# Dealing out the output buffers anew: thirteen stores of up to 30 columns in place of seventeen

## The chip, the cores and the metric

The kernel runs on one core of a Trainium2 chip. The metric is the time of one execution on the device in microseconds, as the median of several runs.

## What is computed

For each of four batches, q, k and v are 6400 x 256 in float32. The attention is over channels: a 256 x 256 matrix per batch, from column norms of q and k over all 6400 rows and their product. A small mixture of experts (two of eight, rank 16) is added to the result.

```
qn = q / (norm(q, axis=1) + 1e-6);  kn = k / (norm(k, axis=1) + 1e-6)
a  = softmax(kn.T @ qn / tau)            # 256 x 256 for each batch
x  = v @ a                               # 6400 x 256 for each batch
y  = x + sum over the two best experts e of w_e * (x @ A[e]) @ B[e]
```

## The kernel before, in words

**Columns and tiles.** The 6400 rows of a batch lie over 128 partitions, 50 rows on each, and the code calls these 50 places columns. A column is 256 numbers on 128 partitions. Work on v and on the output goes in tiles of ten columns: tile (b, i) is batch b (0 to 3), piece i (0 to 4), so there are twenty.

**Three stages for each batch.** First q and k are loaded (in two halves of 25 columns, cast to bf16 in the transfer) and PE sums their products into a Gram matrix (`do_G`), while ACT and DVE make the squares for the norms (`do_sq`, `do_add`, `do_red`). Then a short chain makes the matrix a (`do_rsqrt`, `do_exp`, `do_aT`, `do_waA`). Then each tile of v is loaded (also cast), transposed on PE (`do_T`, L976), multiplied for the gate (`do_ZL`, L1000), gated (`m1` to `g2`; `th` is a Tanh on ACT, L1053), and multiplied for the output (`do_Y`, five products of two columns for each tile, L1103 and L1108). `do_Ye` (through `copy`, L956) copies each product from PSUM to the output buffer. PSUM has two banks for the Gram sums and six for all else; a product that waits for its copy holds one of the six.

**Who decides the order.** A planner in Python (`make_plan`, `Plan.run`) lists the steps once; each engine then runs its own in that order and waits on semaphores. A few steps are put elsewhere by hand (`BEHIND`, `TURNS`). The loads are issued by POOL and share queue q0, in their order. The stores are issued by SP (`do_store`, L1119) on queue q1, in their order: SP stands at each until its data is there, and the later stores stand behind it.

**The output buffer.** `Y` has seven slots of ten columns in float32. `at["y", (b, i)]` says which slot a tile gets; the planner deals the slots out, and two tiles that are stored together (`PAIRS`) get neighbours. The first copy of a tile waits until the store that last read its slot has landed. `HOLD` holds a store back until a named load has landed. Slots 0 to 2, 5 and 6 serve other data at the very start.

The stores of before, with the time at which SP issued each and at which it landed (S1 is the first):

| store | tiles | columns | held until | issued | landed |
|---|---|---|---|---|---|
| S1 | (0,4) | 10 | | 116.54 | 129.94 |
| S2 | (0,1) (0,2) | 20 | v(1,3-4) landed | 129.64 | 147.92 |
| S3 | (1,4) | 10 | | 168.00 | 181.74 |
| S4 | (0,3) | 10 | k of batch 3, second half, landed | 180.91 | 193.73 |
| S5 | (1,2) | 10 | the same | 181.29 | 196.64 |
| S6 | (1,0) (1,1) | 20 | v(2,4) landed | 184.64 | 205.70 |
| S7 | (1,3) | 10 | v(3,0-1) landed | 193.61 | 213.03 |
| S8 | (2,2) | 10 | | 205.37 | 218.07 |
| S9 | (0,0) | 10 | v(3,2-3) landed | 210.86 | 221.66 |
| S10 | (2,0) (2,1) | 20 | the same | 211.24 | 227.51 |
| S11 | (2,3) (2,4) | 20 | | 218.44 | 233.55 |
| S12 | (3,0) | 10 | | 224.53 | 236.61 |
| S13 | (3,1) | 10 | | 230.63 | 239.64 |
| S14 | (3,2) | 10 | | 234.45 | 242.67 |
| S15 | (3,3) | 10 | | 239.46 | 245.70 |
| S16 | (3,4), first 6 | 6 | | 242.97 | 247.53 |
| S17 | (3,4), last 4 | 4 | | 244.28 | 248.75 |

Where nothing stands under "held until", or the hold had long ended, the store waited for the last copy of its tiles.

The last loads of before, on POOL:

| load | columns | issued | landed |
|---|---|---|---|
| v(2,0-1) | 20 | 123.19 | 156.90 |
| v(2,2-3) | 20 | 132.39 | 163.31 |
| q of batch 3, second half | 25 | 148.38 | 170.87 |
| k of batch 3, second half | 25 | 148.89 | 180.90 |
| v(2,4) | 10 | 158.85 | 184.63 |
| v(3,0-1) | 20 | 170.26 | 193.55 |
| v(3,2-3) | 20 | 195.94 | 210.84 |
| v(3,4) | 10 | 206.11 | 217.34 |

Of the kernel before, what the change touches and what calls it, by code (L numbers as in the profile page):

```python
# [15 lines left out]
ACT = mybir.ActivationFunctionType  # L16
# [263 lines left out]
def held_by(p, b, i):  # L280

    kind, d, j = HOLD[b, i]
    return [k for k in p.steps if k[:4] == ("load", kind, d, load_of(d, j) if kind == "v" else j)][-1]
# [167 lines left out]
def make_order(words):  # L451

    order = [("qk", 0, i) for i in range(len(QK))]
    for w in words.split():
# [10 lines left out]
HOLD = {(0, 0): ('v', 3, 2), (0, 1): ('v', 1, 4), (0, 2): ('v', 1, 2), (0, 3): ('k', 3, 1), (1, 0): ('v', 2,  # L465
        4), (1, 1): ('k', 3, 2), (1, 2): ('k', 3, 1), (1, 3): ('v', 3, 1), (2, 0): ('v', 3, 3), (2, 1):
        ('k', 2, 0), (2, 2): ('v', 1, 3), (2, 3): ('v', 2, 2), (3, 3): ('v', 2, 2)}
# [7 lines left out]
WHOLE = {(0, 0): 5, (3, 1): 25}  # L475
V_AT = {(3, 0): 0, (3, 1): 1, (3, 2): 2, (3, 3): 3, (3, 4): 0}
BEHIND = {("sq", "q", 1, 3): ("accs", 0, 0), ("red", "k", 3): ("add", "k", 3, 5),
          ("load", "v", 3, 1, 10, 10): ("T", 2, 3, 2)}
TURNS = [[(x, "k", 3, 5), (x, "q", 3, 8), (x, "q", 3, 9)] for x in ("sq", "add")]
SPLIT, SHARES = set(), ()  # L480
OFF = {(0, 0, 'k'), (0, 0, 'q'), (0, 1, 'k'), (0, 2, 'k'), (0, 2, 'q'), (0, 3, 'k'), (0, 4, 'k'), (0, 4,
# [102 lines left out]
def kernel(  # L584
# [11 lines left out]
    nc = tc.nc  # L596
# [3 lines left out]
    CC = C // P  # L600
# [23 lines left out]
    W = {}  # L624
# [3 lines left out]
    def y_slot(n):  # L628
        return Y[:, n * PC:(n + 1) * PC, :]
# [30 lines left out]
    steps = plan.run(HEAD)  # L660
# [5 lines left out]
    for key, other in BEHIND.items():  # L666
        s = next(s for s in steps if s.key == key)
        steps.remove(s)
        steps.insert(next(n for n, x in enumerate(steps) if x.key == other) + 1, s)
    at = {(kind, name): n for s in steps for kind, name, n in s.got}  # L670
    at.update({("v", name): n for name, n in V_AT.items()})
    loaded, waiting = {}, []

    held = {}

    def sb(s, kind, name, shape, dtype, part=""):

        if (kind, name, part) not in held:
            held[kind, name, part] = sbuf.tile(
                shape, dtype, tag=f"{kind}{at[kind, name]}{part}", name=f"{kind}{part}")  # L680
        return held[kind, name, part]
# [5 lines left out]
    st = [dict() for _ in range(B)]  # L687
# [13 lines left out]
    def do_load(s, what, b, i, c, n):  # L701
        if what == "v":
            t, src = VS[:, at["v", (b, c // PC)] * PC:, :], v_v
        elif c + b:
            t = sb(s, "qk", (what, b, i), [P, max(n for _, n in QK), C], BF16)[:, c - QK[i][0]:, :]
            src = {"q": q_v, "k": k_v}[what]
        else:
            sb(s, "qk", (what, b, i), [P, max(n for _, n in QK), C], BF16)
            lo = "qk".index(what) * n
            W[what] = y_slot(0)[:, lo:lo + n, :]  # L710

            early.append((nc.sync if what == "q" else nc.scalar).dma_start(
                W[what], {"q": q_v, "k": k_v}[what][b, :, 0:n, :]))
            return
        r = P
        if what != "v" and (b, i) == REST:
            if c + n == NC:
                t, n, c, r = held["qk", (what, b, i), ""][:, REST_AT - QK[i][0]:, :], NC - REST_AT, REST_AT, FULL
            else:
                n = REST_AT - c  # L720
                for w in "qk" if what == "q" else "":
                    nc.gpsimd.indirect_dma_start(
                        W["side" + w].rearrange("p c d -> p (c d)"), None,
                        {"q": q, "k": k}[w].rearrange("b n d -> (b n d)").rearrange("(m w) -> m w", w=SIDE * C),
                        bass.IndirectOffsetOnAxis(ap=W["slots"], axis=0), bounds_check=B * N // SIDE - 1, oob_is_err=False)
        if what != "v" and (b, i) in WHOLE:
            if c > WHOLE[b, i]:
                loaded[s.key] = loaded[s.key[:4] + PARTS[b, i][-2]]
                return
            n = sum(QK[i]) - c  # L730
        if what == "v" and (b, i) in WITH_NEXT:
            waiting.append((s.key, at["v", (b, c // PC)], c, n))
            return
        keys = [s.key]
        if what == "v" and waiting:
            key, slot, c0, n0 = waiting.pop()
            assert c0 + n0 == c and slot + n0 // PC == at["v", (b, c // PC)]
            t, c, n = VS[:, slot * PC:, :], c0, n0 + n
            keys.append(key)
        name = nc.gpsimd.dma_start(t[0:r, 0:n, :], src[b, 0:r, c:c + n, :]).ins.name  # L740
        for key in keys:
            loaded[key] = name

    def make_side():

# [156 lines left out]

    def do_exp(s, b, ic):

        nc.scalar.activation(st[b]["exp"][:, ic, :].rearrange("i (cc g p) -> i cc g p", cc=CC, g=4),
                             st[b]["accs"][:, ic, :].rearrange("i (p g cc) -> i cc g p", cc=CC, g=4), ACT.Exp,
                             bias=W["neg"][:, 0:1], scale=st[b]["rk"][:, ic:ic + 1],
                             accum_out=st[b]["sum"][:, ic:ic + 1])

    def do_recip(s, b):  # L910
        st[b]["recip"] = bat.tile([P, CC], FP32, name="recip")
# [40 lines left out]
                                    scalar1=st[b]["recip"][:, ic:ic + 1], scalar2=None, op0=OP.mult)  # L952

    def copy(s, out, in_):
        if s.on == "ACT":
            nc.scalar.copy(out, in_)  # L956
        else:
            nc.vector.tensor_copy(out, in_)

    def do_cast(s, what):  # L960
        nc.scalar.copy(held["qk", (what, 0, 0), ""][:, 0:PARTS[0, 0][0][1], :], W[what])
# [26 lines left out]
    def gate_tiles(s, b, i):  # L988
        for part in ("log", "ga", "gb"):
            sb(s, "gate", (b, i), [P, PC, E], FP32, part)  # L990
        for part in ("m1", "m2", "msum"):
            sb(s, "gate", (b, i), [P, PC], FP32, part)
# [30 lines left out]
    def gate_step(name):  # L1023
        def f(s, b, i):
            if (b, i) in MERGED and name == "m1":
                gate_tiles(s, b, i)
            g = {part: held["gate", (b, i), GATE.get(part, part)]
                 for part in ("log", "m1", "eq1", "lm", "m2", "msum", "t", "th", "mask", "g2")}
            if (b, i) in MERGED:
                g["log"] = held["zl", (b, i), ""][:, :, 0:E]  # L1030
            wide = [P, PC, E]
            if name == "m1":
                nc.vector.tensor_reduce(out=g["m1"], in_=g["log"], axis=AX.X, op=OP.max)
            elif name == "eq1":
                nc.vector.tensor_tensor(out=g["eq1"], in0=g["log"], in1=g["m1"].to_broadcast(wide),
                                        op=OP.is_equal)
            elif name == "lm":
                nc.vector.scalar_tensor_tensor(out=g["lm"], in0=g["eq1"], scalar=-1e30, in1=g["log"],
                                               op0=OP.mult, op1=OP.add)
            elif name == "m2":  # L1040
                nc.vector.tensor_reduce(out=g["m2"], in_=g["lm"], axis=AX.X, op=OP.max)
            elif name == "mask":
                nc.vector.tensor_tensor(out=g["mask"], in0=g["log"], in1=g["m2"].to_broadcast(wide),
                                        op=OP.is_ge)
            elif name == "msum":
                nc.vector.tensor_tensor(out=g["msum"], in0=g["m1"], in1=g["m2"], op=OP.add)
            elif name == "t":

                nc.vector.scalar_tensor_tensor(out=g["t"], in0=g["log"], scalar=2.0,
                                               in1=g["msum"].to_broadcast(wide),  # L1050
                                               op0=OP.mult, op1=OP.subtract)
            elif name == "th":
                nc.scalar.activation(g["th"], g["t"], ACT.Tanh, scale=0.5)  # L1053
            else:

                nc.vector.scalar_tensor_tensor(out=g["g2"], in0=g["th"], scalar=1.0, in1=g["mask"],
                                               op0=OP.add, op1=OP.mult)
        return f
# [55 lines left out]
    def do_store(s, b, i, c, n):  # L1114
        lo = i * PC + c
        at_y = at["y", (b, i)] * PC + c
        p = 0
        for rows in SHARES if (b, i) in SPLIT else (P,):
            r = nc.sync.dma_start(out_v[b, p:p + rows, lo:lo + n, :], Y[p:p + rows, at_y:at_y + n, :])  # L1119
            if (b, i) in HOLD and not p:  # L1120
                tc.add_manual_dep(r.ins, loaded[held_by(plan, b, i)],
                                  mybir.DependencyInfo(mybir.DependencyClass.Sync, mybir.DependencyReason.DATA),
                                  reason="held")
            p += rows
# [3 lines left out]
              exp=do_exp, recip=do_recip, aT_ps=do_aT_ps, aT=do_aT, waA_ps=do_waA_ps, waA=do_waA,  # L1128
# [57 lines left out]
```

## Time and profile before

| | us |
|---|---|
| median of 3 runs | 250.2 (250.02 to 250.29) |
| the profiled execution | 250.12 |
| its span on the page (first to last instruction) | 245.8 |
| landing of the last store, from the span's start | 248.75 |

Times in the text are microseconds from the start of the span. The span ends before the last stores land: 248.75 is 2.95 after its end, and 250.12 is 1.37 after that.

| engine | busy us | share of the span |
|---|---|---|
| PE, matmuls | 212.3 | 86% |
| DVE | 185.7 | 76% |
| ACT | 169.2 | 69% |
| POOL | 23.4 | 10% |

The profile cuts the span into 40 slices and gives the busy share of each engine, and of the 16 DMA engines together, in tenths. A DMA packet in it is what one partition's part of a transfer moves; a store or load over 128 partitions has 128 of them, 8 on each DMA engine. For a load the size counted is that of the bf16 written, half of the float32 read. In the timeline a bracket tells how long the engine was idle before the instruction and what released it.

### The profile page before, as it was taken

The numbers are of one execution on the slowest core, as the hardware profiler recorded it, in microseconds if no ns is written. First come the engines' busy times: TensorE is split into PE (matmuls) and PEld (weight loads), VectorE is DVE, ScalarE is ACT, GpSimd is POOL, SyncE is SP. The second block draws the span as 40 slices with busy tenths as digits, with TensorE's granted clock in tenths as the row PEclk, the third lists the DMA queues.
The fourth block names the chain that finished last, engine by engine and source line by source line (L and its number), as shares of the span: only waits on it lengthen the run. The fifth ranks groups of instructions, "written<-read, shape, count | busy, mean of one in ns | idle before, by whom it ended". The sixth has DMA issues, their size and how long they took to land.

```text
span 245.8 us, 5336 instructions
## 1 busy us (share of the span) xinstructions
PE 212.3 (86%) x2203; PEld 177.4 (72%) x2023; DVE 185.7 (76%) x514; ACT 169.2 (69%) x316; POOL 23.4 (10%) x54
## 2 busy tenths in 40 slices
PE   0309797678998999999968999899999999999996
PEld 0207573267777998879858788799775799999985
DVE  1027789447869789999977889998969878788681
ACT  3729341445766769888787668899453599988875
POOL 7700203000030012000100001000000000000000
PEclk9999999569999999999999999999999999999999
DMA  8999999999999999999999999999999999999999
GB/s 280 218 210 218 215 222 219 209 219 223 206 218 217 221 204 221 223 210 210 257 292 240 337 280 210 218 216 223 277 248 290 401 373 282 313 421 435 406 425 424
DMA packets 7872, 65.93 MB, mean 268 GB/s; under 512 B 1088, under 2 KB 1472, under 8 KB 3368
## 3 DMA queue, kind: packets, MB, share of 16 engines
q0 software_dynamic: 4864, 38.67, 75.0%
q1 hardware_dynamic: 2648, 26.13, 25.6%
q10 hardware_dynamic: 336, 0.79, 0.8%
q8 instruction: 16, 0.26, 0.4%
q14 instruction: 8, 0.07, 0.1%
HBM read 79.90 MB, written 26.21 MB: 432 GB/s over the span
## 4 chain that ended last, share of the span: by engine, by line
DMA 47%; PE 33%; issue 9%; POOL 4%; DVE 4%; ACT 2%; POOLq 0%
DMA v<-in_v_dram 37%; DMA qk<-in_k_dram 10%; PE Y_ps L1103 9%; PE T_ps L976 5%; PE ZL_ps L1000 5%; PE Y_ps L1108 4%; PE acc L785 4%; PE gzT_ps L1090 3%; POOL qk L740 2%; DVE ssq L819 2%; DVE gz L1078 1%; PE acc L789 1%; PE acc L793 1%; ACT y L956 1%; ACT sq L812 1%
## 5 line engine op out<-in xcount | busy, mean ns | idle before, releaser
L785 PE MATMUL acc<-qk 128*128 128x256 bf16 (+1 forms) x400 | 75.4, 284 | 19.8 <-DMA qk<-in_k_dram 11.6
L785 PEld LDWEIGHTS <-qk 128*128 128x128 bf16 (+1 forms) x400 | 38.9, 103 | 32.1 <-DMA qk<-in_k_dram 12.7
L956 ACT COPY y<-Y_ps 128x512 f32<-128x512 f32 x87 | 50.7, 594 | 15.2 <-PE Y_ps L1108 12.8
L1103 PE MATMUL Y_ps<-a_bf,vT 128*128 128x256 bf16 x400 | 60.0, 272 | 0.0
L1103 PEld LDWEIGHTS <-vT 128*128 128x128 bf16 x400 | 38.3, 98 | 4.8 <-issue 0.2
L819 DVE TENSOR_TENSOR ssq<-ssq,sq 128x1280 f32<-128x1280 f32 x25 | 37.2, 1487 | 3.8 <-ACT sq L812 3.7
L1108 PE MATMUL Y_ps<-ball,gzT 128*128 128x256 bf16 x200 | 38.2, 273 | 0.0
L812 ACT ACTIVATE sq<-qk 128x1280 f32<-128x1280 bf16 x25 | 32.1, 1285 | 8.0 <-DVE ssq L819 7.6
L1078 DVE TENSOR_TENSOR gz<-zl,gatega 128x256 bf16<-128x256 f32 x95 | 35.4, 445 | 0.5
L789 PE MATMUL acc<-qk 128*128 128x128 bf16 (+1 forms) x170 | 31.2, 220 | 0.0
L976 PE MATMUL T_ps<-ident,v 128*128 128x128 f32 x200 | 25.8, 275 | 5.8 <-DMA v<-in_v_dram 5.6
L793 PE MATMUL acc<-qk 128*128 128x128 bf16 (+1 forms) x200 | 28.6, 226 | 0.0
L976 PEld LDWEIGHTS T_ps<-ident,v 128*128 128x128 f32 x200 | 21.7, 141 | 7.3 <-issue 4.6
L819 DVE TENSOR_TENSOR ssq<-ssq,y 128x1280 f32<-128x1280 f32 (+1 forms) x10 | 14.8, 1491 | 16.0 <-ACT y L812 15.6
L956 ACT COPY vT<-T_ps 128x512 f32<-128x512 f32 (+1 forms) x47 | 22.7, 547 | 5.9 <-PE T_ps L976 5.6
L1000 PE MATMUL ZL_ps<-waA_sb,vT 128*128 128x136 bf16 x380 | 26.3, 223 | 0.5 <-ACT y L956 0.3
L1000 PEld LDWEIGHTS <-vT 128*128 128x128 bf16 x380 | 23.8, 98 | 1.5 <-DVE gz L1078 0.5
L793 PEld LDWEIGHTS <-qk 128*128 128x128 bf16 (+1 forms) x200 | 19.0, 102 | 4.8
L956 ACT COPY zl<-ZL_ps 128x408 f32<-128x408 f32 (+1 forms) x50 | 19.9, 457 | 3.4 <-PE ZL_ps L1000 3.4
L1090 PE MATMUL gzT_ps<-ident,gz 128*128 128x128 f32 x100 | 19.6, 280 | 2.0 <-DVE gz L1078 1.7
L1108 PEld LDWEIGHTS <-gzT 128*128 128x128 bf16 x200 | 19.5, 98 | 2.3
L812 ACT ACTIVATE y<-qk 128x1280 f32<-128x1280 bf16 (+1 forms) x10 | 12.2, 1263 | 11.4 <-DMA qk<-in_k_dram 8.1
(93 smaller groups left out, 234.9 us busy)
## 6 DMA issues: line engine op xcount, KB each, us to landing
out_dram<-y SPq DMA_DIRECT2D x11, 1280.0 KB, 12.7
out_dram<-y SPq DMA_DIRECT2D x4, 2560.0 KB, 17.3
qk<-in_q_dram POOLq DMA_DIRECT2D x6, 1600.0 KB, 18.1
qk<-in_k_dram POOLq DMA_DIRECT2D x6, 1600.0 KB, 25.4
v<-in_v_dram POOLq DMA_DIRECT2D x6, 1280.0 KB, 29.7
v<-in_v_dram POOLq DMA_DIRECT2D x8, 640.0 KB, 25.6
qk<-in_q_dram POOLq DMA_DIRECT2D x1, 1280.0 KB, 10.9
qk<-in_k_dram POOLq DMA_DIRECT2D x1, 1280.0 KB, 16.4
```

The source lines that it names most:

```text
L785: nc.tensor.matmul(acc[ic][:, 0:256], kt[0:r, j, ic::CC], qt[0:r, j, :], start=c == 0, stop=False, skip_group_check=True)
L789: nc.tensor.matmul(acc[ic][:, 256:384], kt[0:r, j, ic::CC], kt[0:r, j, ic::CC], start=False, stop=False, skip_group_check=True)
L793: nc.tensor.matmul(acc[ic][:, 384:512], qt[0:r, j, ic * P:(ic + 1) * P], qt[0:r, j, ic * P:(ic + 1) * P], start=False, stop=c == NC - 1, s ...
L812: nc.scalar.activation(out[0:r, 0:n, :], t[0:r, j:j + n, :], ACT.Square)
L819: nc.vector.tensor_tensor(out=t, in0=t, in1=held["sq", (w, b, g), ""][0:r, 0:n, :], op=OP.add)
L956: nc.scalar.copy(out, in_)
L976: nc.tensor.matmul(ps[:, j, :], vt[:, c + j, :].bitcast(FP32), W["ident32"], is_transpose=True, start=(j == 0), stop=(j == n - 1))
L1000: nc.tensor.matmul(ps[:, j, :], vT_of(b, i, c + j)[:, :, ic], st[b]["waA"][:, ic, :], start=(j == 0 and ic == 0), stop=(j == n - 1 and ic ...
L1078: nc.vector.tensor_tensor(out=pairs[:, h].rearrange("p c (e r) -> p c e r", e=E), in0=z[:, 2 * h:2 * h + 2, :].rearrange("p c (e r) -> p c ...
L1090: nc.tensor.matmul(ps[:, j, :], pairs[:, j * P:(j + 1) * P], W["ident32"], is_transpose=True, start=(j == 0), stop=(j == n // 2 - 1))
L1103: nc.tensor.matmul(ps[:, j, :], vT_of(b, i, c + j)[:, :, ic], st[b]["a"][:, ic, :], start=(j == 0 and ic == 0), stop=False, skip_group_che ...
L1108: nc.tensor.matmul(ps[:, j, :], pair[:, :, j], W["B"], start=False, stop=(j == 1), skip_group_check=True)
```

## The change

Slots, sizes and holds of the stores are set by hand, on top of the planner's order. `Y_AT` gives each tile a slot. `GOES` renames a store step of the planner (its place in the order stays) or drops it. `AFTER` makes a store, or one load, wait for the end of a named load or of a named ACT instruction; `made` remembers those instructions. The orders of the instructions on PE, DVE and ACT, and those of the loads on POOL, stay as they were; what differs there is which semaphores some copies wait for.

| store | tiles | columns | slots | held until |
|---|---|---|---|---|
| A1 | (0,0) | 10 | 2 | v(1,1) landed |
| A2 | (0,1) (0,2) | 20 | 3, 4 | v(1,3-4) landed |
| A3 | (0,3) (0,4) | 20 | 5, 6 | `th` of tile (2,2) done |
| A4 | (1,0) (1,1) | 20 | 0, 1 | the same |
| A5 | (1,2) (1,3) | 20 | 2, 3 | `exp` of batch 3, first half, done |
| A6 | (1,4) | 10 | 4 | v(3,2-3) landed |
| A7 | (2,0) (2,1) | 20 | 5, 6 | the same |
| A8 | (2,2) (2,3) (2,4) | 30 | 0, 1, 2 | its data |
| A9 | (3,0) (3,1) | 20 | 3, 4 | its data |
| A10 | (3,2) | 10 | 5 | its data |
| A11 | (3,3) | 10 | 6 | its data |
| A12, A13 | (3,4) | 6, 4 | 0 | its data |

One load is held too: v(3,0-1), which waited for the last transpose out of its slots before, now waits for `th` of tile (2,3) as well.

```diff
 BEHIND = {("sq", "q", 1, 3): ("accs", 0, 0), ("red", "k", 3): ("add", "k", 3, 5),
-          ("load", "v", 3, 1, 10, 10): ("T", 2, 3, 2)}
+          ("load", "v", 3, 1, 10, 10): ("th", 2, 3), ("store", 1, 3, 0, 10): ("exp", 3, 0)}
+Y_AT = {(0, 0): 2, (0, 1): 3, (0, 2): 4, (0, 3): 5, (0, 4): 6, (1, 0): 0, (1, 1): 1, (1, 2): 2, (1, 3): 3, (1, 4): 4,
+        (2, 0): 5, (2, 1): 6, (2, 2): 0, (2, 3): 1, (2, 4): 2, (3, 0): 3, (3, 1): 4, (3, 2): 5, (3, 3): 6, (3, 4): 0}
+GOES = {(0, 4): (0, 0, 0, 10), (1, 4): None, (0, 3): (0, 3, 0, 20), (1, 2): None, (1, 3): (1, 2, 0, 20),
+        (2, 2): (1, 4, 0, 10), (0, 0): None, (2, 3): (2, 2, 0, 30), (3, 0): None, (3, 1): (3, 0, 0, 20)}
+AFTER = {("store", 0, 0): ("load", "v", 1, 1, 10, 10), ("store", 0, 3): ("th", 2, 2), ("store", 1, 2): ("exp", 3, 0), ("store", 1, 0): ("th", 2, 2),
+         ("store", 1, 4): ("load", "v", 3, 2, 20, 20), ("load", "v", 3, 1): ("th", 2, 3)}
...
+    for s in list(steps):
+        if s.key[0] == "store" and s.key[1:3] in GOES:
+            if GOES[s.key[1:3]]:
+                s.key = ("store",) + GOES[s.key[1:3]]
+            else:
+                steps.remove(s)
     at = {(kind, name): n for s in steps for kind, name, n in s.got}
     at.update({("v", name): n for name, n in V_AT.items()})
-    loaded, waiting = {}, []
+    at.update({("y", name): n for name, n in Y_AT.items()})
+    loaded, waiting, made = {}, [], {}
+
+    def behind(ins, key):
+        if key in AFTER:
+            other = AFTER[key]
+            tc.add_manual_dep(ins, loaded[other] if other[0] == "load" else made[other],
+                              mybir.DependencyInfo(mybir.DependencyClass.Sync, mybir.DependencyReason.DATA), reason="held")
+        return key in AFTER
...
-        name = nc.gpsimd.dma_start(t[0:r, 0:n, :], src[b, 0:r, c:c + n, :]).ins.name
+        ins = nc.gpsimd.dma_start(t[0:r, 0:n, :], src[b, 0:r, c:c + n, :]).ins
+        behind(ins, s.key[:4])
         for key in keys:
-            loaded[key] = name
+            loaded[key] = ins.name
...
             r = nc.sync.dma_start(out_v[b, p:p + rows, lo:lo + n, :], Y[p:p + rows, at_y:at_y + n, :])
-            if (b, i) in HOLD and not p:
+            if not behind(r.ins, s.key[:3]) and (b, i) in HOLD:
                 tc.add_manual_dep(r.ins, loaded[held_by(plan, b, i)],
```

`do_exp`, `copy` and the `th` branch of `gate_step` change only in that they note the name of their instruction in `made`.

More of the change, by code (lines that the diff above doesn't have):

```diff
@@ L903, in do_exp @@
     def do_exp(s, b, ic):
[L905 to L908, printed above, removed]
+        made[s.key] = nc.scalar.activation(
+            st[b]["exp"][:, ic, :].rearrange("i (cc g p) -> i cc g p", cc=CC, g=4),
+            st[b]["accs"][:, ic, :].rearrange("i (p g cc) -> i cc g p", cc=CC, g=4), ACT.Exp, bias=W["neg"][:, 0:1],
+            scale=st[b]["rk"][:, ic:ic + 1], accum_out=st[b]["sum"][:, ic:ic + 1]).ins.name
     def do_recip(s, b):
@@ L954, in copy @@
     def copy(s, out, in_):
[L955 to L958, printed above, removed]
+        r = nc.scalar.copy(out, in_) if s.on == "ACT" else nc.vector.tensor_copy(out, in_)
+        made[s.key] = r.ins.name
     def do_cast(s, what):
@@ L1052, in f @@
             elif name == "th":
-                nc.scalar.activation(g["th"], g["t"], ACT.Tanh, scale=0.5)
+                made[s.key] = nc.scalar.activation(g["th"], g["t"], ACT.Tanh, scale=0.5).ins.name
             else:
```

## The prediction

> **What bounds the kernel now.** I read first the page's DMA lines, then PE's waits from 157.5 on, then the stores one by one.
>
> ```profile
> DMA  8999999999999999999999999999999999999999
> GB/s 280 218 210 218 215 222 219 209 219 223 206 218 217 221 204 221 223 210 210 257 292 240 337 280 210 218 216 223 277 248 290 401 373 282 313 421 435 406 425 424
> ...
> q0 software_dynamic: 4864, 38.67, 75.0%
> q1 hardware_dynamic: 2648, 26.13, 25.6%
> ...
> DMA 47%; PE 33%; issue 9%; POOL 4%; DVE 4%; ACT 2%; POOLq 0%
> ```
>
> The 16 DMA engines are full in every slice but the first. q0 (loads, counted at half their float32 bytes) and q1 (stores) take 75.0% and 25.6%, together the whole span. So the last landing, 248.75, is the sum of all transfers: a store moved elsewhere moves others, and the end stays unless bytes pass faster or the engines run dry.
>
> PE is the second bound. Its last wait for data in the timeline, and all its waits from 157.5 to 244:
>
> ```profile
> 157.03 1.06 PE L976 MATMUL T_ps<-ident,v 128*128 128x128 f32 x8 [1.00 <-DMA v<-in_v_dram]
> ```
> ```profile
> PE gzT_ps L1090 <- DVE gz L1078: 0.6, 2, 0.4
> PE ZL_ps L1000 <- DVE gz L1078: 0.2, 1, 0.2
> ```
>
> After v(2,0-1) lands PE waits 0.8 us in 87 us, and not for a load. What comes late to PE there moves its end, but the stores lag PE: S15 is issued at 239.46, when S13 (239.64) and S14 (242.67) have not landed. I estimate that PE may come 1 us later (0 to 1.2) before the end moves: S17 lands 4.47 after its issue and 1.22 after S16, so 0 to 3 us of the 4.47 are queueing.
>
> **Fewer, larger stores.** Four stores go. The price of a merge comes from landings one behind the other when no load runs: S12 to S15, ten columns each, land 3.03 apart (236.61, 239.64, 242.67, 245.70); S11, twenty columns, lands 6.04 after S10. Two small ones cost 6.06, one large one 6.04: 0.02 saved, for four merges 0.1. The other end: S12 took 3.06, and S10 landed 5.85 after S9, so 0.27 a merge, 1.1 for four. These rows exclude a loss for twenty columns. Thirty no row shows; three tens are 9.09, one and a half twenties 9.06, so it is taken as free. I take 0.1: S10 to S11 is clean of loads, while S9 and S10 were queued when the last load had just ended. SP's issues (0.33 each) lie beside full DMA engines and cost nothing either way.
>
> **Loads and stores at once.** By the DMA view, 40 to 110 (loads only) moved 15.08 MB counted, 30.2 of float32, in 70 us: 431 GB/s. 218 to 233 (stores only, mostly of twenty columns) moved 6.39 MB: 426. 170 to 218, mixed and mostly ten-column stores: 5.34 doubled and 9.60 MB in 48 us, 422. 133 to 146, a twenty-column store against 25-column loads:
>
> ```profile
> q0 software_dynamic: 127, 1.42, 51.4%
> q1 hardware_dynamic: 128, 2.62, 47.7%
> ```
>
> That is 5.46 MB in 13 us, 420. At 431 the stretch 170 to 218 would be 1.0 us shorter, at 420 it would be 0.2 longer. The changed kernel mixes as long but with larger packets; I take -0.1 and keep +0.2 and -1.0.
>
> The same two lines show 127 load packets against 128 store packets: the queues take turns packet by packet, so a twenty-column packet against the same load packet takes a larger share than a ten-column one, and loads beside it are slower. The Trainium skill ("DMA: Bandwidth & Descriptors", Queues, rings and completion order) says that each engine goes round its queues and empties a whole packet of some 9 to 17 descriptors before it switches. With the eight rows that a store has on an engine, a store would go in one turn by that; the trace, at 127 to 128 over 13 us, shows turns of one row.
>
> **Stores and loads that move.** A1 leaves after v(1,1) lands at 117.21 instead of 116.54, A2 at v(1,3-4) as before: the same 30 columns precede v(2,0-1), so 156.90 stands. S3 (168.00) is gone; A3 and A4 start when `th` of (2,2) ends (172.13 + 0.25). A step of each transfer alone: 25 columns 7.55 (163.31 to 170.87), twenty loaded 6.1 (71.65 to 77.78), ten loaded 3.07 (68.58 to 71.65), twenty stored 6.04. k's second half follows q's (170.87): alone it would land at 178.4. A3's first packets come some 3.5 later than its issue (the prefetched loads are ahead, an estimate: at 133, 3.4 after S2's issue, both queues flow), at 176; the last 2.4 us of k at half share take 4.6, so it lands near 180.6 (180.90 before). v(2,4) then alternates with A3: 188 to 190 instead of 184.63, but PE transposes it only at 194.00. v(3,0-1) is issued at `th` of (2,3), 185.91 + 0.25, instead of 170.26. The sum 170.87 + 7.55 + 6.04 + 3.07 + 6.04 + 6.1 puts its landing at 199.7 instead of 193.55; PE wants it at 204.6. On POOL v(3,2-3) stands behind it and goes when its slots are free, as before:
>
> ```profile
> 195.94 0.53 POOL L740 DMA_DIRECT2D v<-in_v_dram  x1 [25.15 <-PE T_ps L976]
> ```
>
> It lands at 207 to 210 (210.84 before), v(3,4) near 217.5 as before. No load reaches PE late.
>
> **New waits of copies.** The first copy of (2,0) now waits for A3, issued 172.4; sharing as above, it lands near 187.5. The first copy is at 186.63 on ACT:
>
> ```profile
> 186.63 0.59 ACT L956 COPY y<-Y_ps 128x512 f32<-128x512 f32 x1
> 193.08 0.37 ACT L841 COPY acc_sb<-acc 128x256 f32<-128x256 f32 x1 [5.86 <-PE acc L789]
> ```
>
> Behind it ACT idles 5.86 anyway, and its PSUM bank is next taken at 192.89 (L834): about 1 us of waiting is hidden; the cover ends near 192. (2,2) waits for A4 (195 to 198.5), its copy is at 199.94. (2,4) waits for A5, issued at 199.5 when `exp` ends: 3.5 to start, 6.04 of its own, 2 to 4 of loads in between, 0.7 to land: 212.2 to 214.3. Its first copy is the one at 214.02:
>
> ```profile
> 214.02 1.24 ACT L956 COPY y<-Y_ps 128x512 f32<-128x512 f32 x2
> 215.43 0.81 ACT L956 COPY zl<-ZL_ps 128x408 f32<-128x408 f32 x2 [0.17 <-PE ZL_ps L1000]
> ```
>
> The bank is taken again by the third product of the tile, at 215.7, so a landing until 215.0 costs PE nothing. The others have 5 us and more. A9 waits for both its tiles, until 230.63, where S12 went at 224.53. 50 columns stand from it to the end, as from S12; all before S12 landed at 233.55, and its data was through some 0.6 earlier. With 1.5 from issue to flow A9 is there at 232.1, 0.8 early.
>
> **Sum.** Merges -0.1, mixture -0.1, waits and dry queues 0: 250.12 - 0.2 = 249.9 (248.0 with both gains at their ends, 250.2 with neither). The profiled execution lies 0.08 below the median 250.2. What can be told from no change is about 0.2%, 0.5 us; so: no change.
>
> **Rivals.**
> *The transfers pass faster.* Merges at 0.13 (midway) save 0.5, and half the gain of an unmixed stretch another 0.5: 249.1. For it: 422 GB/s against 431. Against: the landings 3.03 and 6.04, and that A3 to A7 still run against loads. That it goes beyond 249.1 I give 0.08 of its chance. 0.25.
> *Tile (2,4) waits for A5* (slower). One store of twenty columns lands 15.1 to 21.1 after its issue before (S11, S6), if queued behind others; at 18.3 (S2, alone in q1 against loads) A5 would land at 217.8, ACT would stand 3.8 at the copy with the zl copies, the gate and the other y copies behind it, PE would lose 2.8 and, less 1 of spare, the end 1.8: 251.9. At 217 it is 251.1. It decides from 215.0, the end moves from 216. Against: less load work beside A5 than beside S2. 0.15.
> *The queues run dry* (slower). v(3,0-1) is through near 199.1 and v(3,2-3), issued 195.94, must flow by then; A9 must by 232.9. Each has about 0.8 of spare; if PE or the loads are off by 1.8 at one, the DMA engines stand for 1 us that nothing gives back: 250.9. 0.12.
> *A whole store in one turn.* A3 and A4, 12.1 together, would pass ahead of k: 178.4 + 12.1 = 190.5, while PE starts on it near 183.5 (25 columns of 0.33 before 193.05, and 1.2 of other work): 7 less 1 of spare, 255.9. The page's rule above would do that; the packet counts speak against it. 0.01.
>
> **How the numbers follow.** The forecast has 0.47. Faster by over 0.5 us: 0.25. Slower by over 0.5: 0.15 + 0.12 + 0.01 = 0.28. The range goes from 249.1, the faster rival, to 251.1, the tile wait at 217 and the dry queue; below lie 0.08 and above about 0.1. The forecast's own range is 249.7 to 250.4.
>
> **What would show it right or wrong.** Right: thirteen stores, DMA at 9 in every slice, PE's waits after 157.5 near 1 us, k's second half at 180 to 181, A5 landed before 215, the first copy of (2,0) waiting under 2 us. Wrong: a gap on PE after 214 ended by an ACT copy (the tile wait), DMA slices under 9 near 199 or 232 (dry), or landings of the pure stores less than 3.0 per ten columns (faster).

## The result, and the profile after

The changed kernel takes 251.97 us (median of 6 runs, 251.62 to 252.52), the kernel before 250.12 (6 runs, 250.02 to 250.29): a ratio of 1.0075, 95% interval 1.0062 to 1.0088. It is 1.9 us slower, beyond the range of the prediction (249.1 to 251.1). The profiled execution took 251.81; its span is 246.0, and its last store lands at 250.46, 1.71 later than before.

First the page of the changed kernel, the lines that answer to those shown of before: the busy share of the DMA engines and the rate in 40 slices of 6.15 us, the two queues, the chain.

```profile
DMA  8999999999999999999999999999999999999999
GB/s 280 217 211 216 211 226 221 206 221 219 210 221 216 217 206 223 217 218 206 243 289 276 325 271 215 216 218 219 256 357 398 267 197 322 338 407 438 422 411 424
...
q0 software_dynamic: 4864, 38.67, 75.4%
q1 hardware_dynamic: 2023, 25.83, 25.1%
...
PE 42%; DMA 36%; issue 9%; DVE 6%; POOL 4%; ACT 3%; POOLq 0%
```

The DMA engines are at 9 in every slice but the first, as before, and the packets of both queues again take the whole span (75.4 and 25.1%). By this line nothing is lost, and yet the last store lands later. One slice of the rate stands out: the 33rd, 196.8 to 202.9, with 197 GB/s. In slices 2 to 19, before the first store, the rate of loads alone is 206 to 226.

Next the waits of PE from 157.5 to 250, and two stretches of ACT in the timeline, around the first copies of (2,0) and of (2,4):

```profile
PE gzT_ps L1109 <- DVE gz L1097: 0.6, 2, 0.4
PE Y_ps L1122 <- DVE zl L976: 0.2, 1, 0.2
```
```profile
187.00 0.59 ACT L976 COPY y<-Y_ps 128x512 f32<-128x512 f32 x1
193.40 0.37 ACT L862 COPY acc_sb<-acc 128x256 f32<-128x256 f32 x1 [5.82 <-PE acc L810]
...
214.34 1.24 ACT L976 COPY y<-Y_ps 128x512 f32<-128x512 f32 x2
215.75 0.81 ACT L976 COPY zl<-ZL_ps 128x408 f32<-128x408 f32 x2 [0.17 <-PE ZL_ps L1019]
```

PE waits 0.8 us, as before. The copy of (2,0) is at 187.00 (186.63 before) and that of (2,4) at 214.34 (214.02), neither with an idle time in front of it. The computation is where it was, some 0.3 later; what is late is the stores. A13 is issued at 244.60 and lands at 250.46, 5.86 later, where S17 took 4.47.

Now the stretch of the low slice, in the view by windows: the last two columns are the mean busy share of the DMA engines and the GB/s. First before, then after.

```profile
196.00:200.00 4.00, 4.00 (x39) 3.61 (x38) 2.53 (x10) 3.83 (x9) 0.46 (x1) 1.00 1.01 427
200.00:204.00 4.00, 4.00 (x52) 3.75 (x50) 3.80 (x12) 3.63 (x10) 0.00 (x0) 1.00 1.01 294
```
```profile
196.00:200.00 4.00, 4.00 (x39) 3.62 (x38) 2.46 (x11) 3.82 (x10) 0.53 (x1) 1.00 1.01 204
200.00:204.00 4.00, 4.00 (x52) 3.75 (x50) 4.00 (x12) 3.67 (x10) 0.00 (x0) 1.00 1.03 174
```

The rates can't be compared across these rows as they stand, since a load counts half of its float32 bytes. The DMA view of 196 to 204 splits them by queue (packets, MB, share of the 16 engines), before and after:

```profile
q1 hardware_dynamic: 128, 2.32, 68.5%
q0 software_dynamic: 53, 0.54, 32.0%
```
```profile
q0 software_dynamic: 162, 1.50, 101.5%
q1 hardware_dynamic: 1, 0.00, 0.0%
```

In float32 that is 2.32 + 2 x 0.54 = 3.40 MB in 8 us before, 425 GB/s, and 3.00 MB after, 375. The 0.40 MB that are missing cost 0.94 us at 425. In the changed kernel no store flows here: the data of A4 is through at 195.5, and A5, issued at 199.85, moves its first packet at 204.05. What flows is the end of v(3,0-1), which lands at 199.57, and v(3,2-3), issued at 196.25:

```profile
196.25 0.53 POOL L760 DMA_DIRECT2D v<-in_v_dram  x1 [8.95 <-PE T_ps L995]
```

The trace's packets show two things. First, some engines stand for a moment. With 16 engines, fewer than 16 packets in flight means that at least one has none; in the kernel before that does not happen from 190 to 244, and in the changed kernel 15 and at the lowest 14 are in flight at times between 197.0 and 203.3. What is missing adds up to 1.3 us of one engine, less than 0.1 us of all sixteen, too little to show in the slices. Second, and this is most of it, the packets take longer. One partition's row of a twenty-column load takes 0.78 us in the mean in the kernel before (190 to 211). In the changed kernel the 147 rows that start between 196 and 204.6 take 0.89, and the 38 of them from 201.5 on 1.10, up to 1.41.

The other part of the 1.71 us is at the end. The packets of a store are spread over 16 engines, and it lands when the slowest is done. By the completions of the last store in the trace, the mean engine was done at 249.20, against 248.32 before: 0.88 later, near the 0.94 above. It was done 1.26 before the slowest, against 0.43 before: 0.83 more, which makes up the 1.71. Where this uneven end comes from is open. Slow packets are not needed for it: E1 and E10 below move 428 and 429 GB/s over 196 to 208, and still their mean engine ends 0.75 and 1.40 before the slowest. In E10 the engines had even been level at 220, where the completions of A6 lie within 0.19.

### The profile page after: what moved, and what is told of

It is laid out like the page before. It is cut to its first block, busy times and chain, and to the rows that moved or that the text cites. A ratio compares the mean times of both kernels' runs of the same rounds, so it can differ in the third digit from the quotient of the medians.

```text
span 246.0 us, 5327 instructions
## 1 busy us (share of the span) xinstructions
PE 214.8 (87%) x2203; PEld 179.5 (73%) x2023; DVE 184.9 (75%) x514; ACT 169.0 (69%) x316; POOL 23.7 (10%) x54
## 3 DMA queue, kind: packets, MB, share of 16 engines
q0 software_dynamic: 4864, 38.67, 75.4%
q1 hardware_dynamic: 2023, 25.83, 25.1%
## 4 chain that ended last, share of the span: by engine, by line
PE 42%; DMA 36%; issue 9%; DVE 6%; POOL 4%; ACT 3%; POOLq 0%
DMA v<-in_v_dram 28%; PE Y_ps L1122 11%; DMA qk<-in_k_dram 8%; PE acc L806 6%; PE T_ps L995 6%; PE Y_ps L1127 5%; PE ZL_ps L1019 5%; PE gzT_ps L1109 3%; PE acc L810 2%; DVE gz L1097 2%; DVE ssq L840 2%; POOL qk L760 1%; PE acc L814 1%; ACT y L976 1%; ACT zl L976 0%
## 5 line engine op out<-in xcount | busy, mean ns | idle before, releaser
L806 PE MATMUL acc<-qk 128*128 128x256 bf16 (+1 forms) x400 | 76.3, 287 | 19.3 <-DMA qk<-in_k_dram 11.2
L806 PEld LDWEIGHTS <-qk 128*128 128x128 bf16 (+1 forms) x400 | 39.4, 104 | 31.8 <-DMA qk<-in_k_dram 12.1
L995 PE MATMUL T_ps<-ident,v 128*128 128x128 f32 x200 | 27.4, 286 | 3.7 <-DMA v<-in_v_dram 3.3
L995 PEld LDWEIGHTS T_ps<-ident,v 128*128 128x128 f32 x200 | 23.2, 147 | 5.0 <-issue 4.1
L814 PEld LDWEIGHTS <-qk 128*128 128x128 bf16 (+1 forms) x200 | 19.2, 103 | 4.9
## 6 DMA issues: line engine op xcount, KB each, us to landing
qk<-in_k_dram POOLq DMA_DIRECT2D x6, 1600.0 KB, 25.1
```

Source lines behind the costliest of these rows:

```text
L806: nc.tensor.matmul(acc[ic][:, 0:256], kt[0:r, j, ic::CC], qt[0:r, j, :], start=c == 0, stop=False, skip_group_check=True)
L814: nc.tensor.matmul(acc[ic][:, 384:512], qt[0:r, j, ic * P:(ic + 1) * P], qt[0:r, j, ic * P:(ic + 1) * P], start=False, stop=c == NC - 1, s ...
L995: nc.tensor.matmul(ps[:, j, :], vt[:, c + j, :].bitcast(FP32), W["ident32"], is_transpose=True, start=(j == 0), stop=(j == n - 1))
```

## Experiments

Each kernel was timed beside the kernel before, whose median there was 250.41 for E1 to E7 and 250.52 for E8 to E10; ratios are to that. The views are of one execution of each. Theories named in the expectations: **L**, any load without a store beside it is slow; **S**, the large stores are dear in themselves; **W**, waits of the computation set the time. Later **T** and **D** came in place of L: T, the tail of a load with nothing behind it and nothing beside it is slow; D, a load that starts on engines which have nearly run dry, with no store beside it, is slow.

**E1: A5 issued earlier.** One hold is changed; A5 goes at 186.36 instead of 199.85.

```diff
-("store", 1, 2): ("exp", 3, 0)
+("store", 1, 2): ("th", 2, 3)
```

> The changed kernel, but A5 waits for th of tile (2,3) (near 187) instead of exp of batch 3 (near 200); it is then queued behind A4. Theory L (the load v(3,2-3) crosses with no store beside it, its packets are slow, and the DMA engines lose about 1.0 us between 196 and 204): that stretch moves near 427 GB/s of float32 again instead of 380, and the time falls by 1.0 to 1.7, to 250.3 to 251.0; some may come back at v(3,4), which then crosses with little beside it. Theory S (stores of 20 and 30 columns are dear in themselves, one DMA engine falling behind on them): no change, 251.9. Theory W (waits on the compute engines): no change, 251.9.

Measured: 250.32 (250.09 to 250.74), ratio 1.0000, interval 0.9991 to 1.0010. The whole loss is gone, with the same thirteen stores, so S and W, which both said 251.9, fall, and what the loss needs is the place of A5 in time. The DMA view of E1 over 196 to 204:

```profile
q1 hardware_dynamic: 93, 1.80, 53.1%
q0 software_dynamic: 96, 0.82, 48.7%
```

3.44 MB in 8 us, 430 GB/s. But L has a first crack here. Once the data of A5 is through (207.8), E1's loads run alone too, and the row of the windows shows them at 209 GB/s, 418 in float32, where the changed kernel had 174:

```profile
208.00:212.00 4.00, 4.00 (x48) 3.75 (x46) 2.71 (x9) 3.27 (x7) 0.00 (x0) 1.00 1.01 209
```

**E2: A5 and A6 both earlier.** A6, too, no longer waits for v(3,2-3); it goes when `exp` ends.

```diff
-("store", 1, 2): ("exp", 3, 0), ("store", 1, 4): ("load", "v", 3, 2, 20, 20)
+("store", 1, 2): ("th", 2, 3), ("store", 1, 4): ("exp", 3, 0)
```

> As the run before, and A6 waits for exp of batch 3 instead of the landing of v(3,2-3), so that a store stands in the queue beside every load to the end. Theory L: 250.0 to 250.4, as the kernel before the change. Theory S or W: 251.9.

Measured: 251.40 (251.27 to 252.04), 1.0045 (1.0028 to 1.0061). The slow stretch is gone, but the time is not back, and no theory had forecast it. Stores now take a share from the loads as long as they last; v(3,2-3) lands at 214.07 instead of 208.86, and PE waits for it:

```profile
PE T_ps L995 <- DMA v<-in_v_dram: 2.4, 2, 1.6
```

The last store is issued at 246.44, 1.84 later. So the cure has a limit on the other side: too many stores beside the loads make PE the late one.

**E3: the stores from A3 on in pieces of ten columns**, one behind the other at the same holds; the pieces of A8 and A9 go as their tiles are ready, so the first of A8 leaves before its last tile is there.

```diff
-r = nc.sync.dma_start(out_v[b, p:p + rows, lo:lo + n, :], Y[p:p + rows, at_y:at_y + n, :])
+step = n if (b, i) == (0, 1) else PC
+for x in range(0, n, step):
+    m = min(step, n - x)
+    r = nc.sync.dma_start(out_v[b, p:p + rows, lo + x:lo + x + m, :], Y[p:p + rows, at_y + x:at_y + x + m, :])
```

> The changed kernel with its slots and holds, but every store from A3 on goes out in pieces of ten columns, one behind the other at the same releases (A8 and A9 in pieces as their tiles are ready). Theory S: back to 250.1 to 250.6. Theory L: the lone crossing of v(3,2-3) stays, 251.7 to 252.2, with 196 to 204 near 380 GB/s.

Measured: 252.18 (251.98 to 252.33), 1.0072 (1.0056 to 1.0089). Small stores lose as much as large ones: S is refuted again.

**E4: v(3,2-3) as two loads of ten columns**, issued one behind the other.

```diff
-ins = nc.gpsimd.dma_start(t[0:r, 0:n, :], src[b, 0:r, c:c + n, :]).ins
+if s.key[:4] == ("load", "v", 3, 2):
+    nc.gpsimd.dma_start(t[0:r, 0:PC, :], src[b, 0:r, c:c + PC, :])
+    ins = nc.gpsimd.dma_start(t[0:r, PC:n, :], src[b, 0:r, c + PC:c + n, :]).ins
```

> The changed kernel, but v(3,2-3) goes as two loads of ten columns issued one behind the other. If the slow packets come from there being one single transfer on the queue (nothing to fetch ahead), a second load behind it should help and the time falls by 0.5 or more, to 251.4 or less; if they come from loads alone after the engines ran dry, whatever their number, it stays at 251.7 to 252.2.

Measured: 252.06 (251.82 to 252.74), 1.0076 (1.0056 to 1.0097). Nothing is won by two loads: it is no matter of how a single large transfer is cut.

**E5: ten columns from A5 into A4.** Still thirteen stores and the same moments of issue; A4 has thirty columns and A5 ten.

```diff
-(1, 3): (1, 2, 0, 20)
+(1, 3): (1, 3, 0, 10), (1, 0): (1, 0, 0, 30)
-("store", 1, 2): ("exp", 3, 0)
+("store", 1, 3): ("exp", 3, 0)
```

> The ten columns of tile (1,2) move from A5 into A4, so A4 is thirty columns, issued at 173.25, and A5 ten, issued at 199.85 as before this edit. The same bytes go out; 3 us more of stores flow ahead of 199, so v(3,0-1) should land near 202.5 instead of 199.57, with v(3,2-3) (issued 196.25) already queued behind it, and A5 should begin near 203.5 to 204. So loads still run alone for some 3 us, near 200.5 to 204, but the tail of the one has the next behind it. Theory T (a load loses speed only in its last 3 us, where nothing is queued behind it and no store runs beside it): 250.1 to 250.7, with 425 to 430 GB/s in 196 to 204. Theory L (any load without a store beside it is slow): 251.3 to 252.0, with 380 to 400 GB/s where the loads are alone.

Measured: 250.53 (250.33 to 251.46), 1.0006 (0.9996 to 1.0016). The loss is gone from the median, although A5 goes no earlier (199.85). The profiled execution is the slowest of the ten (251.46): PE waited 1.0 there for a copy on DVE, and the last store was issued at 245.76, 1.16 later than in the changed kernel. Its load stretch shows no slow packets all the same. There v(3,0-1) lands at 203.17, so v(3,2-3), issued at 196.25, finds the queue full. Between 200 and 203 the loads run alone, at 2 x 0.65 MB in 3 us, 433 GB/s:

```profile
q0 software_dynamic: 79, 0.65, 102.4%
q1 hardware_dynamic: 5, 0.00, 0.2%
```

L is refuted: being alone does not make a load slow. (The loads alone over 40 to 110 before, at 431, had said so already.) But most of these rows are of v(3,0-1), issued at 186.78, whose mean engine is done at 202.2; v(3,2-3) is alone for a short time only, since A5 flows from 203.2.

**E6: the hold of v(3,0-1) undone**; that load is issued at 170.34 again.

```diff
-("load", "v", 3, 1, 10, 10): ("th", 2, 3)
+("load", "v", 3, 1, 10, 10): ("T", 2, 3, 2)
-("load", "v", 3, 1): ("th", 2, 3)
```

> The changed kernel with only the hold of v(3,0-1) undone: it waits again for the last transpose out of its slots, and is issued near 170. Theory H (the hold of the load makes the loss): 250.0 to 250.5. Theories T and L: what is issued by 196 is the same sum and is moved by about 199.5 in either order; v(3,2-3), issued near 196, begins near 200 and has no store beside it until A5 begins near 203.5. Under L 251.5 to 252.0 (3.5 us at about 380 GB/s lose 0.4, engines with nothing to move near 199.5 as much again). Under T its tail lies beside A5, and the loss is less: 250.7 to 251.4.

Measured: 251.70 (251.45 to 252.25), 1.0061 (1.0044 to 1.0078). Most of the loss stays, so the hold of the load is not its cause. Only the order of the same work changed: v(3,0-1) landed at 199.88, v(3,2-3) was issued at 195.98, and no store flowed until 203.0. T had expected 250.7 to 251.4 and missed.

**E7: A5 issued some 4 us earlier**, at 195.61, held by a copy of the transposes of tile (2,4), which ends near that time.

```diff
-("store", 1, 2): ("exp", 3, 0)
+("store", 1, 2): ("Te", 2, 4, 0)
```

> The changed kernel with A5 held by the copy of tile (2,4) on ACT that ends near 195.7 instead of by the exp that ends near 199.8: A5 is issued near 196, 3.9 earlier, and begins near 199.5, together with v(3,2-3). The tail of v(3,0-1), 197 to 199.5, is still alone; the tail of v(3,2-3) has A5 beside it. T and L: most of the loss returns, 250.1 to 250.8, with 400 to 425 GB/s in 196 to 204. Theory W (the time is set by waits on PE and the copies, not by the transfers): unchanged, 251.8 to 252.2.

Measured: 251.13 (250.46 to 251.59), 1.0035 (1.0023 to 1.0048). About half of the loss is won back, less than expected. The profiled run is the fastest of the six (250.46) and shows no slow packets, with A5 flowing from 197.2. It can't say what the slower runs lost. That stays open.

**E8 and E9: one more load behind v(3,2-3).** Ten columns of v are read again, into a buffer of k that nobody reads any more. E8 is the changed kernel with that load, E9 is E1 with it.

```diff
+if s.key[:3] == ("load", "v", 3) and c == 20:
+    nc.gpsimd.dma_start(held["qk", ("k", 3, 1), ""][:, 0:10, :], v_v[3, :, 40:50, :])
```

> The changed kernel with one more load of ten columns issued right behind v(3,2-3); it reads rows of v again into a buffer of k that nobody reads any more. The output stays the same; the bytes cost 3.0 us (ten columns). v(3,2-3) still starts on an empty queue with no store beside it, but its tail now has a load behind it. Theory T (the tail of a load with nothing behind it and nothing beside it is slow): 425 to 430 GB/s in 200 to 204, and the loss of the change goes: 253.0 to 253.8, that is 250.1 plus 3.0 and a few tenths. Theory D (a load that starts on engines that have run dry, with no store beside it, is slow): 360 to 400 GB/s in 200 to 204, 254.4 to 255.0.

> The control for the run before: the kernel whose A5 is held by th of tile (2,3), with the same redundant load behind v(3,2-3). T and D: it had no loss, so only the bytes count: 250.3 plus 3.0, 253.1 to 253.6. If the redundant load costs more than its bytes (v(3,4) comes 3 us later to PE), it shows here, and the run before is read against this one.

Measured: E8 254.80 (254.04 to 256.06), 1.0163 (1.0146 to 1.0181); E9 253.13 (253.04 to 253.37), 1.0109 (1.0092 to 1.0126). The control pays for its bytes (2.8 more than E1). E8 is 1.67 above it; the changed kernel, from another session, is 1.65 above E1. The loss has not moved, though the tail of v(3,2-3) now has a load behind it. T is refuted; D had expected 254.4 to 255.0. The row of E8 by windows:

```profile
200.00:204.00 4.00, 4.00 (x49) 3.72 (x47) 4.00 (x12) 3.66 (x10) 0.00 (x0) 1.00 1.04 177
```

A full share and 177 GB/s again; from 198 to 200 up to four of the engines stand. The 131 twenty-column rows that start from 197.5 to 206 take 0.97 us in the mean, up to 1.8; from 206 on, A5 having flowed since 205.0, they take 0.78 again. The additional load comes later: its rows start at 208.2 and take the usual 0.40 of ten columns. This profile is of the slowest of the four executions (256.06, in which PE waited 1.8 for a load), so its numbers are the far end of E8.

**E10: a lone tail in another place.** E1, with A6 waiting for v(3,4), the last load, so that nothing runs beside that load's end.

```diff
-("store", 1, 4): ("load", "v", 3, 2, 20, 20)
+("store", 1, 4): ("load", "v", 3, 3, 40, 10)
+BEHIND: ("store", 2, 2, 0, 10): ("load", "v", 3, 3, 40, 10)
```

> The kernel whose A5 is held by th of tile (2,3) has no loss. Here its A6 (and with it A7, behind it on SP) waits for v(3,4), the last load, in place of v(3,2-3): A6 is issued near 215 in place of 211.9, so that the last 3 us of v(3,4), 212 to 215, have nothing behind them and no store beside them. T: the slow tail comes back at this place, 330 to 400 GB/s in 212 to 215 where 425 was, and v(3,4) lands near 215.5. Theory P (the slowness belongs to v(3,2-3) or to 196 to 204, not to a lone tail): 425 there, v(3,4) lands at 214.7 to 215.0. In both, the engines then stand for some 3.4 us until A6 begins, and all later stores come that much later: 253.5 to 254.0 under P, 254.0 to 255.0 under T.

Measured: 253.46 (253.29 to 253.71), 1.0118 (1.0101 to 1.0135), and v(3,4) lands at 215.51. By its time this is P, by the landing T. Over 212 to 215 the queue moved 0.43 MB, 287 GB/s in float32, even less than T expected. The rows by windows say of what kind that is:

```profile
208.00:212.00 4.00, 4.00 (x48) 3.71 (x47) 2.75 (x9) 3.31 (x8) 0.00 (x0) 1.00 0.98 205
212.00:216.00 4.00, 4.00 (x45) 3.69 (x43) 3.52 (x13) 3.71 (x10) 0.00 (x0) 1.00 0.52 106
```

The rate falls here with the busy share (0.98 to 0.52): the engines finish at different times and then stand, and every row of v(3,4) takes the usual 0.40 us of ten columns. That is how a queue that runs dry looks. In the changed kernel the share stayed at 1.03 while the rate was 174.

**All runs by one measure.** "Lead" is the time from the issue of v(3,2-3) to the landing of the load ahead of it. The rate is in float32 over 196 to 208, from the trace's packets, each one's bytes spread evenly over its duration (the DMA view counts a packet where it starts, which shifts a stretch by up to 0.3 MB at an edge).

| kernel | lead, us | store beside it in 200 to 203 | GB/s | time |
|---|---|---|---|---|
| before | -2.4 | yes | 428 | 250.1 to 250.5 |
| after | 3.3 | no | 389 | 251.97 |
| E3 | 3.6 | no | 397 | 252.18 |
| E4 | 3.7 | no | 400 | 252.06 |
| E6 | 3.9 | no | 408 | 251.70 |
| E8 | 3.3 | no | 362 | 254.80, of it 3.0 for bytes (profiled run 256.06) |
| E7, profiled run | 4.7 | yes | 428 | 250.46 (median 251.13) |
| E5 | 6.9 | no | 429 | 250.53 (profiled run 251.46) |
| E1 | 7.7 | yes | 428 | 250.32 |
| E2 | 7.7 | yes | 428 | 251.40 (PE waits) |
| E9 | 7.8 | yes | 428 | 253.13, of it 3.0 for bytes |

In these runs two conditions meet where the loss is: a short lead and no store beside. With either missing (before: the queue already empty, but stores beside; E5: alone, but 6.9 of lead) the rate is 428 or 429; with both it is 408 or less, and the less the shorter the lead. The packets in flight part the same runs: between 196 and 206 they fall under 16 in all five slow kernels, to 12 in E8, and in none of the six others. So the loss goes together with some engines running dry.

Three things stay open. Why the packets last longer is not known. A row's time may itself hold waiting: in E4 the first four rows of v(3,2-3), which can be told by their size, begin from 197.48 on, take 0.62 to 1.48 instead of 0.40, and all end between 198.6 and 199.0. That the load's packets are handed out late, and an engine waits with a row begun, is a rival that no run tested. Nor is the place excluded (P): all the slow rows lie between 197 and 206, at v(3,0-1) and v(3,2-3). Last, a long lead by itself may not be enough. In E10 v(3,4), 6.0 ahead and with nothing beside it, is not slow, but the second half of E4's v(3,2-3), issued 6.3 before the first landed, has rows of up to 1.15 until A5 flows.

No version beats the kernel before: E1 and E5 equal it. E1's DMA engines, like those of before, are full from 220 to the end, so a new order of the same bytes seems to have little left to win. (E5's profile, the slow one, has them run dry near 233.)

## Why the prediction was wrong

**The step that failed** is "waits and dry queues 0" in the sum. The prediction saw the place: "v(3,0-1) is through near 199.1 and v(3,2-3), issued 195.94, must flow by then", with 0.8 of spare. Two things were wrong in it. It took one moment, 199.1, for all 16 engines; in the changed kernel their completions of v(3,0-1) lie between 197.36 and 199.57, and from 197.0 on, 0.7 after the issue of v(3,2-3), some have nothing in flight. And it counted as a loss only the time in which engines stand, which by the packets in flight is less than 0.1 us here. The longer rows, which it did not think of, make nearly all of the 0.9 in bytes. With the 0.83 of the uneven end the term of 0 measured 1.71; why the end is uneven, and why the rows take longer, stays open.

**The rivals.** *The queues run dry* had the right spot and the right side, and part of the mechanism, for one or two engines did stand. But its sign, slices under 9 near 199 or 232, did not come, since standing engines were not where the time went, and its price (250.9) was too low. *Tile (2,4) waits for A5* gave 251.9, nearly the time that came, for a wait that did not come: A5 landed at 213.83, within the forecast 212.2 to 214.3, and its copy went on time. The right number there is chance. (The terms printed for that forecast add up to 211.7 to 213.7, so the landing lies 0.1 beyond them.) *The transfers pass faster* did not happen, and *a whole store in one turn* neither: over 133 to 146 the two queues moved packet for packet in the changed kernel as well. Equal counts alone would also fit turns of several rows; but A2 took from 132.7 to 146.3 for rows that take 6.04 alone, so it did not go in one turn.

```profile
q0 software_dynamic: 132, 1.48, 53.7%
q1 hardware_dynamic: 131, 2.58, 47.0%
```

**What held.** The estimates of arrival: k's second half at 179.76 (180.6 forecast, 180 to 181 as the sign), A3 at 186.97 (187.5), v(3,0-1) at 199.57 (199.7), v(3,2-3) at 208.86 (207 to 210), v(2,4) at 188.98 (188 to 190). No load reached PE late, and PE's waits are 0.8 again. Merging stores is worth next to nothing, as the 0.1 said: E3, which undoes the merges from A3 on, is 0.2 us from the changed kernel, within the spread of either. A9 was issued at 230.94, at its data, and the queue before it did not run dry. The 1.5 from issue to flow that its spare rests on is shown by no row; in E2, where the engines had run dry, A9's first packet came 0.83 after its issue.

**What the profile of before could have told.** The prediction took the rate of loads alone from 40 to 110, 431 GB/s, where several were issued ahead. The one load of before that found its queue empty after the start, v(3,2-3), had S6 and S7 flowing beside it (0.65 MB of stores and 0.53 of loads over 200 to 204). No row showed a load with a short lead and nothing beside it, and the rate of 431 was carried over to it without a bound; that was the place for a wider range. The same load also shows a start that the spare of 0.8 left no room for: issued at 195.94, while stores flowed, it moved its first packet at 199.97, 4.03 later, where the spare of 0.8 leaves 2.4.

## What to carry to other kernels

A DMA share of 9 in every slice tells that the engines hold packets, not that they move bytes: read GB/s by queue, in the bytes of one side, for each stretch, and compare them with a stretch of the same mix. When stores are moved or held, look for the stretch that they leave: there a store should run beside the next load, or the load should be issued well before the one ahead is through (in this place 6.9 us went without loss and 3.9 did not; how much is enough is not shown). Too much beside it is dear as well: in E2 the loads came so late that PE waited.

## What was not expected of the hardware

A load in that state keeps nearly all 16 engines taken: 1.04 of share with 177 GB/s and never under 15 rows in flight (E8, 200 to 204), against 1.01 with 209 (E1, 208 to 212), both with loads alone.

How long a store takes to begin depends on what the engines hold. A5, issued on an empty store queue while loads flowed, moved its first packet 4.2 later, and A1, A2 and A3 took 3.4; A6 in E10, issued at 215.52 when the engines stood, began 0.8 later. The Trainium skill ("DMA: Bandwidth & Descriptors", Specifications) gives some 0.6 us to the first byte for a DMA issued from SP. The trace comes near that only where the engines stood (0.8); with loads in flight some 3 us more pass.
